# Attention scores as pairs of 64-row TensorE tiles, with unpadded keys and another share-out of PSUM

## Chip, cores, metric

One core of a Trainium2 chip. The metric is the device time of one execution in microseconds, slowest core (here the only one). The kernel before: 403.52 us, median of 4 runs (401.85 to 407.54).

## The reference, cut to what matters

```python
# batch 8, heads 8, 576 positions, head_dim 64; d_model 512, d_ff 2048
scores = q @ k^T / 8 + bias_table[bucket(|i - j|)]     # per batch and head
attn   = softmax(scores) @ v
x      = attn.transpose(0, 2, 1, 3).reshape(4608, 512)
h      = x @ w_in
out    = (h + sin(alpha * h)**2 / alpha) @ w_out
```

## The kernel before

Everything is fp16 with fp32 accumulation. A planner in Python keeps a list of tasks per engine and emits them in the order of a modelled time, so each engine's instruction order is fixed when the kernel is built. Three kinds of work share TensorE (PE below): **scores** and attention times values (**av**) of batch t; **hidden** matmuls (x by w_in) of a block of 512 rows; and **mo** matmuls (g by w_out, where g is h + sin(alpha * h)**2 / alpha), which have the lowest priority and go wherever nothing else is ready. The vector engine (DVE) applies the bias and does most of the copying. The exp runs on the scalar engine (ACT) in an *exp stage* per batch, the sine in a *sin stage*; a table load lies between them.

The heads have 64 channels, but the array has 128 rows. Two heads lie above one another in a tile of 128 partitions, and the keys are padded with zeros, so that one 128-row matmul gives one head's scores:

```python
# kz: [128, 4 pairs, 2*576]; head 0 in rows 0..63 of the first half, head 1 in rows 64..127 of the second
units = [(0, c) for c in range(4)] + [(1, 0), (2, 0), (2, 2)]     # 7 a pair of heads
for z in range(2):                                                # a unit fills one two-bank PSUM tile
    for y in range(1 if kind == 0 else 2):
        k0 = S * z + 128 * (c + y)
        q0, n = WIN[0 if kind == 0 else 1]                        # WIN = ((0, 384), (384, 192))
        full(sc.v[:, z, n*y : n*y + n], kz[:, p, k0 : k0 + 128], qT[:, p, q0 : q0 + n], True, True)
...
nc.scalar.activation(out=o, in_=x, func=AF.Exp, scale=0.125)      # one exp of 768 a unit, 576 for the tail
```

The last 64 keys of both heads (the *tail*, `kt`) share one 128-row matmul. PSUM: two score tiles of two banks each, two banks for av, two for mo. In the sin stages the score banks hold the hidden matmuls' results.

The softmax here doesn't subtract the row's maximum and nothing guards it: scores larger than these inputs give would overflow.

Of the kernel before, what the change touches and what calls it, by code (L numbers as in the profile page):

```python
# [34 lines left out]
NBUF = {"sc": 4, "av": 2, "mo": 2, "u": 3, "g": 2, "s16": 3, "sq": 3, "outs": 5, "xn": 3, "xp": 5}  # L35


class Task:
    def __init__(self, engs, emit, deps, pri, nb=0.0):
        self.engs, self.emit, self.deps, self.pri, self.nb = engs, emit, list(deps), pri, nb  # L40
        self.allocs = []
        self.s_only = self.fill = False
        self.end = self.eng = None


class Buf:
    def __init__(self, tag):
        self.tag, self.users = tag, []
# [6 lines left out]
class Plan:  # L55


    def __init__(self):
        self.tasks = []
        self.sin = self.in_qk = False  # L60
        self.used = self.share = 0
        self.warm = None
        self.rings = {k: [] for k in NBUF}

# [9 lines left out]
    def ready(self, t):  # L74
        r = t.nb
# [8 lines left out]
        for b in t.allocs:  # L84
            ring, n = self.rings[b.tag], NBUF[b.tag]
            k = taken[b.tag] = taken.get(b.tag, -1) + 1
            if len(ring) + k >= n:
                for x in ring[k - n].users:
                    if x.end is None:
                        return None  # L90
                    r = max(r, x.end)
        return r

    def run(self, t0):
        free = {e: t0 for e in ("PE", "ACT", "DVE", "POOL", "DMA", "SP")}
        todo = list(self.tasks)
        while todo:
# [30 lines left out]
            if e == "PE" and self.warm is not None and free[e] < WARM_END:  # L128
                ring = self.rings["mo"][-2:]
                b = Buf("mo")  # L130
                x = Task({}, None, [], 0)
                b.users.append(x)
                if st > free[e] + 0.5 and len(ring) == 2 and all(
# [5 lines left out]
                    self.rings["mo"].append(b)  # L139
                    continue  # L140
            if t.fill:
                self.used += 1
                st -= FILL_GAP
                fin -= FILL_GAP
            for b in t.allocs:
                self.rings[b.tag].append(b)
# [13 lines left out]
D_FLIP = 3.0  # L160
T_START = 7.0
# [30 lines left out]
def kernel(  # L192
# [46 lines left out]
    kzs = [sgl.tile([128, NP, 2 * S], F16, name=f"kz{i}") for i in range(2)]  # L239
    kraw = sgl.tile([128, NP, S], F16, name="kraw")  # L240
# [75 lines left out]
    banks = [0]  # L316
    halves = {}

    def new_sc(n):
        z = banks[0] // 2 % 2  # L320
        m, pool = halves.get(z, (0, None))
        if m != n:
            if pool is not None:
                pool.release()
            pool = tc.alloc_tile_pool(
                name=f"sc{banks[0]}", bufs=1, space=bass.MemoryType.PSUM,
                side="right" if z else "left", reuse_waits="tile",
            )
            halves[z] = (n, pool)
        banks[0] += n  # L330
        if n == 1:
            return pool.tile([128, 512], F32, name="sc", tag="sc", bufs=2)
        return pool.tile([128, 2, 512], F32, name="sc", tag="sc", bufs=1)

    def new_av():
        return ps.tile([128, 512], F32, name="av", tag="av", bufs=NBUF["av"])

    def new_mo():
        return ps.tile([128, 512], F32, name="mo", tag="mo", bufs=NBUF["mo"])
# [8 lines left out]
    def load_kqT(t):  # L348
        nc.sync.dma_start_transpose(out=kraw[:, :, :], in_=staged_k.ap()[t])
        kz = kzs[t % 2]  # L350
        nc.sync.dma_start(out=kz[0:64, :, 0:S], in_=kraw[0:64, :, :])
        nc.sync.dma_start(out=kz[64:128, :, S : 2 * S], in_=kraw[64:128, :, :])
        for z in range(2):
            r = slice(64 * z, 64 * z + 64)
            nc.sync.dma_start(out=kts[t % 2][r, :, r], in_=kraw[r, :, 512:S])
        nc.sync.dma_start_transpose(out=qTs[t % 2][:, :, :], in_=staged_q.ap()[t])

# [47 lines left out]
    def clear(eng, i):  # L405
        eng.memset(kzs[i][0:64, :, S : 2 * S], 0.0)
        eng.memset(kzs[i][64:128, :, 0:S], 0.0)
# [11 lines left out]
    def warm(n):  # L419
        x = new_mo()  # L420
# [53 lines left out]
    eps_ = new_mo()  # L474
# [34 lines left out]
    def plan_tr(t, p, kq, pri, nb, deps=()):  # L509

        b, c = Buf("mo"), Cell()
        far = kq == 0 and (t == 1 or p > FAR)

        def mm(e):
            c.v = new_mo().bitcast(F16)
# [15 lines left out]
        def cp(e):  # L531
            pin = c.v[:, 0:S].rearrange("d (i p) -> d p i", i=SI)

            def put(dst, r):
                copy_on(e, dst.rearrange("d (p i) -> d p i", i=SI)[r], pin[r])

            if kq == 1:
                put(qTs[t][:, p, :], slice(0, 128))
            elif far:
                put(kraw[:, p, :], slice(0, 128))  # L540
            else:
                put(kzs[t][:, p, 0:S], slice(0, 64))
                put(kzs[t][:, p, S : 2 * S], slice(64, 128))

        m = plan.add({"PE": 0.4 if t == 0 and p == 0 else 0.5}, mm, deps, pri, nb, new=[b])
        eng = {"DVE": 0.75, "ACT": 0.72} if kq or far else {"DVE": 1.6, "ACT": 1.55}
# [5 lines left out]
        if far:  # L552
            farq.append((p, x))
            if t and p % 2 == 0:
                return [], []
# [4 lines left out]
            def split(e):  # L560
                kz = kzs[t]
                nc.sync.dma_start(out=kz[0:64, p0:p1, 0:S], in_=kraw[0:64, p0:p1, :])
                nc.sync.dma_start(out=kz[64:128, p0:p1, S : 2 * S], in_=kraw[64:128, p0:p1, :])
                for z in range(2):
                    r = slice(64 * z, 64 * z + 64)
                    nc.sync.dma_start(out=kts[t][r, p0:p1, r], in_=kraw[r, p0:p1, 512:S])
# [4 lines left out]
            return [y], [y]  # L571

        def tail(e):
            for z in range(2):
                r = slice(64 * z, 64 * z + 64)
                nc.vector.tensor_copy(
                    out=kts[t][r, p, r], in_=kzs[t][r, p, S * z + 512 : S * z + S]
# [4 lines left out]
    def plan_alpha():  # L582
        b, c = Buf("mo"), Cell()

        def mm(e):
            c.v = new_mo()
# [14 lines left out]
    def plan_pair(t, p, kqt, tails, first, gate, ub):  # L601

        u = Cell()
        done = {}
        units = [(0, c) for c in range(4)] + [(1, 0), (2, 0), (2, 2)]
        head = []
        for i, (kind, c) in enumerate(units):
            b, sc = [Buf("sc"), Buf("sc")], Cell()

            def qk(e, i=i, kind=kind, c=c, sc=sc):  # L610
                if i == 0:
                    if p == 0:
                        first()
                        plan.in_qk, plan.used = True, 0
                        plan.quota = QUOTA.get(t, QUOTA_ELSE)
                    u.v = new_u()
                plan.share = (len(units) * p + i + 1) / (NP * len(units))
                if p == NP - 1 and i == len(units) - 1:
                    plan.in_qk = False
                sc.v = new_sc(2)  # L620
                kz, qT = kzs[t % 2], qTs[t % 2]
                for z in range(2):
                    if kind == 1:
                        full(sc.v[:, z, 0:288], kts[t % 2][:, p, :],
                             qT[:, p, 288 * z : 288 * z + 288], True, True)
                        continue
                    for y in range(1 if kind == 0 else 2):
                        k0 = S * z + 128 * (c + y)
                        q0, n = WIN[0 if kind == 0 else 1]
                        full(sc.v[:, z, n * y : n * y + n], kz[:, p, k0 : k0 + 128],  # L630
                             qT[:, p, q0 : q0 + n], True, True)

            def ex(e, kind=kind, c=c, sc=sc):
                uz = u.v[:, 0:8, :].rearrange("p (z c) q -> p z c q", z=2)
                if kind == 0:
                    o, x = uz[:, :, c, 0:384], sc.v[:, :, 0:384]
                elif kind == 1:
                    o = u.v[:, 8, :].rearrange("p (b q) -> p b q", b=2)
                    x = sc.v[:, :, 0:288]
                else:  # L640
                    o = uz[:, :, c : c + 2, 384:576]
                    x = sc.v[:, :, 0:384].rearrange("p z (c q) -> p z c q", c=2)
                nc.scalar.activation(out=o, in_=x, func=AF.Exp, scale=0.125)  # L643

            base = PB + 100 * (16 * p + 2 * i)
            n = 576 if kind == 1 else 768
            m = plan.add({"PE": n / 2400.0 + 0.01}, qk, kqt + (tails if kind == 1 else []), base,
                         after=head + (list(split_of.values()) if t == 1 else [])
                         + ([aheads[t]] if t in aheads else []), new=b + ([ub] if i == 0 else []))
            head = head or [m]  # L650
            qk_last[:] = [m]
            x = plan.add({"ACT": t_act(n)}, ex, [m] + gate, base + 20, use=b + [ub])
            if kind == 1:

                def bh(e):
                    io = u.v[:, 8, 384:576]
                    nc.vector.tensor_tensor(out=io, in0=io, in1=mh[:, p, 0:192], op=ALU.mult)

                done[(0, 4)] = x
                done[(1, 4)] = plan.add({"DVE": 0.19}, bh, [x], base + 10,  # L660
                                         nb=0.0 if t else T_MH[p > 0], use=[ub])
                continue
            w = 0 if kind == 0 else 1
            q0, n = WIN[w]
            for cc in range(c, c + 1 + w):
                done[(w, cc)] = x
                lo, hi = max(q0, 128 * cc - 128), min(q0 + n, 128 * cc + 256)
# [299 lines left out]
```

## Time and profile before

| | before |
|---|---|
| time, median of 4 | 403.52 us |
| span of the profiled execution | 400.6 us |
| PE / ACT / DVE busy | 97% / 83% / 67% |
| exp stage, batches 4 to 7 | 21.8 us |
| sin stage, batches 3 to 6 | 17.5 us |
| last stretch, after the last exp | 103.8 us |

The prediction below shows the lines of these views. One excerpt more, PE's timeline in an exp stage (start, duration, instruction, count): how a pair's last scores lie among the filler.

```profile
284.42 0.49 PE L417 MATMUL sc<-qT,kz 128*128 128x192 f16 x4
284.75 0.59 PE L417 MATMUL mo<-w_out,g 128*128 128x512 f16 x2
285.18 0.49 PE L417 MATMUL sc<-qT,kz 128*128 128x192 f16 x4
285.51 0.38 PE L417 MATMUL mo<-w_out,g 128*128 128x512 f16 x1
```

A row's duration includes the pipeline's end; what an instruction costs PE is the distance between starts. Four score matmuls of 192 columns take 284.75 - 284.42 = 0.33 us, 82 ns each; the mo matmul from 285.51 is followed at 285.73, 0.22 us later. There is no gap.

### The profile page before, as it was taken

Reading aid. Unit: us, or ns where it says so; the run is one execution under the profiler, and the core shown is the slowest. Engines: PE = TensorE matmul, PEld = TensorE weight load, DVE = VectorE, ACT = ScalarE, POOL = GpSimd, SP = SyncE. Lnnn points to the kernel's source line nnn. Section 1 sums busy time; section 2 is a strip of 40 time slices with the busy share of each in tenths; the row PEclk is TensorE's granted clock in tenths of the full one; section 3 lists DMA queues with packets and bytes.
Section 4 is the critical chain, followed back from the end, with each engine's and each line's share of the span. In section 5 each row is a group of like instructions: output and inputs, shape, how many; then the busy total and the mean of one; then the engine's idle time right before and its main releaser. Section 6 shows DMA issues by size and latency. Waiting matters only on the chain.

```text
span 400.6 us, 8664 instructions
## 1 busy us (share of the span) xinstructions
PE 388.1 (97%) x3398; PEld 221.9 (55%) x3398; DVE 266.5 (67%) x621; ACT 331.6 (83%) x492; POOL 86.2 (22%) x98
## 2 busy tenths in 40 slices
PE   5989999999999999999999999999999999999996
PEld 2466447744777744774477447745764444444442
DVE  5886976777676778678866877687766808519200
ACT  2888999889999999999999999999996818729311
POOL 7962944170009080009000400000000000000000
PEclk9999999999999999999999999999999999999999
DMA  9999999999929999989971946200131020010122
GB/s 169 214 214 221 215 188 142 188 179 156 210 59 110 183 185 155 128 175 128 165 187 33 101 94 167 57 16 28 45 57 41 2 79 26 19 65 22 54 79 79
DMA packets 152808, 46.42 MB, mean 116 GB/s; under 512 B 138104, under 2 KB 147152, under 8 KB 152768
## 3 DMA queue, kind: packets, MB, share of 16 engines
q0 software_dynamic: 89872, 19.04, 57.7%
q1 hardware_dynamic: 62672, 26.79, 32.4%
q8 instruction: 26, 0.43, 0.4%
q14 instruction: 14, 0.11, 0.1%
q10 hardware_dynamic: 224, 0.05, 0.1%
HBM read 37.76 MB, written 16.52 MB: 136 GB/s over the span
## 4 chain that ended last, share of the span: by engine, by line
PE 86%; DMA 5%; ACT 5%; DVE 2%; issue 1%; POOL 0%; ACTq 0%; SPq 0%; DVEq 0%
PE sc L417 44%; PE mo L417 30%; PE av L417 11%; DMA kz<-kraw 2%; ACT s L805 2%; DMA e_dram<-e_sb 1%; DMA phi_sb<-phi_const 1%; ACT u L643 1%; DMA mhr<-e_dram 1%; ACT sq L812 1%; DVE g L819 1%; PE av L764 0%; DVE sq L814 0%; ACT L875 0%; DVE u L674 0%
## 5 line engine op out<-in xcount | busy, mean ns | idle before, releaser
L643 ACT ACTIVATE u<-sc 128x768 f16<-128x768 f32 (+1 forms) x224 | 162.1, 788 | 6.8 <-PE sc L417 4.4
L417 PE MATMUL mo<-w_out,g 128*128 128x512 f16 x576 | 152.6, 379 | 0.0
L417 PE MATMUL sc<-xT,w_in 128*128 128x512 f16 x576 | 132.4, 379 | 0.2 <-DVE g L819 0.2
L819 DVE SCALAR_TENSOR_TENSOR g<-sq,inv_a,sc 128x512 f16<-128x512 f16 x144 | 103.7, 746 | 35.1 <-PE mo L417 25.8
L417 PE MATMUL sc<-qT,kz 128*128 128x192 f16 (+1 forms) x512 | 94.9, 289 | 3.9 <-ACT u L643 1.5
L805 ACT ACTIVATE s<-sc,alphaT 128x512 f16<-128x512 f32 x144 | 93.0, 678 | 6.2 <-PE sc L417 4.9
L674 DVE TENSOR_TENSOR u<-u,m2r 128x512 f16<-128x512 f16 (+1 forms) x192 | 68.8, 389 | 44.0 <-ACT u L643 43.5
L417 PEld LDWEIGHTS <-w_in 128*128 128x128 f16 x576 | 55.1, 98 | 64.3 <-issue 0.5
L417 PEld LDWEIGHTS <-g 128*128 128x128 f16 x576 | 55.8, 98 | 50.8
L417 PEld LDWEIGHTS <-u 128*128 128x128 f16 x1440 | 61.7, 97 | 12.0 <-DVE u L674 0.2
L417 PEld LDWEIGHTS <-kz 128*128 128x128 f16 x512 | 43.3, 98 | 29.4 <-issue 7.4
L417 PE MATMUL av<-v,u 128*128 128x65 f16 x1280 | 59.3, 193 | 0.0
L812 ACT ACTIVATE sq<-s 128x512 f16<-128x512 f16 x78 | 49.0, 629 | 2.8 <-DVE g L819 0.7
L361 POOL DMA_DIRECT2D v<-in_v_dram x24 | 22.2, 1060 | 116.8 <-PE av L417 116.8
L503 ACT ACTIVATE outs<-mo 128x512 f32<-128x512 f32 x18 | 10.7, 597 | 41.7 <-PE mo L417 41.7
L417 PE MATMUL av<-vh,u 128*128 128x130 f16 x160 | 35.1, 220 | 0.0
L814 DVE TENSOR_TENSOR sq<-s 128x512 f16<-128x512 f16 x66 | 27.8, 423 | 8.6 <-ACT s L805 7.8
L727 DVE TENSOR_TENSOR xp<-av,rd 128x384 f16<-128x384 f32 (+1 forms) x48 | 23.6, 491 | 1.7
L875 ACT ACT_TABLE_LOAD x13 | 16.7, 1283 | 0.2
L343 POOL DMA_DIRECT2D staged_q<-in_q_dram x6 | 16.1, 2680 | 1.5 <-DMA staged_q<-in_q_dram 1.5
L726 DVE RECIPROCAL rd<-av 128x6 f32<-128x6 f32 x64 | 11.9, 186 | 4.8 <-PE av L417 4.0
L343 POOL DMA_DIRECT2D staged_k<-in_k_dram x6 | 13.5, 2254 | 3.3 <-DMA staged_k<-in_k_dram 3.3
(74 smaller groups left out, 140.6 us busy)
## 6 DMA issues: line engine op xcount, KB each, us to landing
out_dram<-outs SPq DMA_DIRECT2D x36, 256.0 KB, 2.0
staged_k<-in_k_dram POOLq DMA_DIRECT2D x6, 576.0 KB, 13.2
staged_q<-in_q_dram POOLq DMA_DIRECT2D x6, 576.0 KB, 17.3
kz<-kraw SPq DMA_DIRECT2D x12, 288.0 KB, 6.6
v<-in_v_dram POOLq DMA_DIRECT2D x24, 128.0 KB, 6.5
w_in<-in_moe_w_in_dram POOLq DMA_DIRECT2D x4, 512.0 KB, 8.4
w_out<-in_moe_w_out_dram POOLq DMA_DIRECT2D x4, 512.0 KB, 12.0
w_out<-in_v_dram SPq DMA_DIRECT2D x4, 256.0 KB, 8.7
```

The source lines that it names most:

```text
L343: nc.gpsimd.dma_start(out=dst.ap()[t].rearrange("s (h d) -> s h d", h=H), in_=src[t].rearrange("h s d -> s h d"),)
L361: nc.gpsimd.dma_start(out=vs[t % 2][:, c, :, 0:D], in_=vp[128 * c : 128 * c + 128],)
L417: nc.tensor.matmul(out=out, lhsT=lhsT, rhs=rhs, start=start, stop=stop)
L643: nc.scalar.activation(out=o, in_=x, func=AF.Exp, scale=0.125)
L674: nc.vector.tensor_tensor(out=io, in0=io, in1=m2[:, 2 * p : 2 * p + 2, x0 : x0 + hi - lo], op=ALU.mult,)
L726: nc.vector.reciprocal(out=r, in_=a[:, :, :, D])
L727: nc.vector.tensor_tensor(out=y.rearrange("p c (z d) -> p c z d", z=2), in0=a[:, :, :, 0:D], in1=r.unsqueeze(3).to_broadcast([128, nq, 2, ...
L805: nc.scalar.activation(out=s16.v, in_=h.v, func=AF.Sin, scale=alphaT[:, f : f + 1])
L812: nc.scalar.activation(out=sq.v, in_=s16.v, func=AF.Square)
L814: k_of(e).tensor_tensor(out=sq.v, in0=s16.v, in1=s16.v, op=ALU.mult)
L819: nc.vector.scalar_tensor_tensor(out=gcell[b].v[:, f, :], in0=sq.v, scalar=inv_a[:, f : f + 1], in1=h.v, op0=ALU.mult, op1=ALU.add,)
L875: nc.scalar.preload_act_table_set(name)
```

## The change

Intent: a 64-row matmul uses half of the array, and two on different halves can run together. So each head's scores are computed from its own 64 partitions, without zero padding, and both heads of a unit run side by side. That also does away with the padded copy of the keys. A switch between the full array and row tiles costs something, so from batch 2 on two units are issued as a run; this needs a third score tile, which is taken from the av and mo banks. Units become 512 queries (four a pair) and 64 queries (one a pair), plus the tail.

```diff
-    kzs = [sgl.tile([128, NP, 2 * S], F16, name=f"kz{i}") for i in range(2)]
-    kraw = sgl.tile([128, NP, S], F16, name="kraw")
+    kTs = [sgl.tile([128, NP, S], F16, name=f"kT{i}") for i in range(2)]
     def load_kqT(t):
-        nc.sync.dma_start_transpose(out=kraw[:, :, :], in_=staged_k.ap()[t])
-        kz = kzs[t % 2]
-        nc.sync.dma_start(out=kz[0:64, :, 0:S], in_=kraw[0:64, :, :])
-        nc.sync.dma_start(out=kz[64:128, :, S : 2 * S], in_=kraw[64:128, :, :])
+        kT = kTs[t % 2]
+        nc.sync.dma_start_transpose(out=kT[:, :, :], in_=staged_k.ap()[t])
...
+        if t < LAG - 1:                                   # LAG = 3: batches 0 and 1
+            groups = [[(p, i)] for p in range(NP) for i in (0, 1, 2, 3, "t", 4)]
+            nreg = 2
+        else:
+            groups = [
+                [(y + p, i) for y, i in g] for p in range(0, NP, 2) for g in (
+                    ((0, 0), (0, 1)), ((0, 2), (0, 3)), ((0, "t"),), ((0, 4), (1, 0)),
+                    ((1, 1), (1, 2)), ((1, "t"),), ((1, 3), (1, 4)),
+                )
+            ]
+            nreg = 3
...
+                    for y in range(1 if i < 4 else 4):
+                        q0, n = QW[i == 4]                # QW = ((0, 512), (512, 64))
+                        k0 = 128 * (i if i < 4 else y)
+                        for z in range(2):
+                            r = slice(64 * z, 64 * z + 64)
+                            full(sc.v[:, z, n * y : n * y + n], kT[r, p, k0 : k0 + 128],
+                                 qT[r, p, q0 : q0 + n], True, True)
...
-        mb, ob, m = Buf("mo"), Buf("outs"), Cell()
+        mt = "moE" if b == 0 else "am" if b < T - 2 else "moL"
+        mb, ob, m = Buf(mt), Buf("outs"), Cell()
...
+        if t == LAG - 1:
+            early = early + cps[0] + avs[1] + xdone[(1, 0)] + xdone[(1, 1)]
```

`am` is either of two banks that av and mo share from batch 2 on; `moE` and `moL` are two banks before and three after that time. The last two lines mean that batch 2's scores come only after block 0's mo and batch 1's av are done, because they take over those banks.

## The prediction

> **What bounds the kernel now.** I read the page first: how full each engine is, and who makes the chain that ended last.
>
> ```profile
> PE 388.1 (97%) x3398; PEld 221.9 (55%) x3398; DVE 266.5 (67%) x621; ACT 331.6 (83%) x492; POOL 86.2 (22%) x98
> PE 86%; DMA 5%; ACT 5%; DVE 2%; issue 1%; POOL 0%; ACTq 0%; SPq 0%; DVEq 0%
> L643 ACT ACTIVATE u<-sc 128x768 f16<-128x768 f32 (+1 forms) x224 | 162.1, 788 | 6.8 <-PE sc L417 4.4
> L417 PE MATMUL sc<-qT,kz 128*128 128x192 f16 (+1 forms) x512 | 94.9, 289 | 3.9 <-ACT u L643 1.5
> ```
>
> TensorE makes 86% of the chain. ACT at 83% looks far behind, but that is an average over unlike stages. So next I cut the span at the 13 table loads (each marks a change between an exp stage and a sin stage) and read the busy time of each stretch.
>
> ```profile
> core 0: us, PE busy (x) PEld busy (x) DVE busy (x) ACT busy (x) POOL busy (x), PEclk, DMA share, GB/s
> 235.70:257.50 21.80, 21.80 (x267) 15.07 (x265) 14.55 (x42) 21.53 (x29) 0.00 (x0) 1.00 0.51 125
> 257.50:275.00 17.50, 17.50 (x106) 8.38 (x103) 14.78 (x27) 17.04 (x28) 0.00 (x0) 1.00 0.09 17
> 296.80:400.60 103.80, 100.12 (x486) 45.58 (x482) 45.52 (x80) 54.50 (x88) 0.00 (x0) 1.00 0.14 46
> ```
>
> A batch is an exp stage of 21.8 us and a sin stage of 17.5 us. In both, PE and ACT are full together. The last stretch, 104 us, has PE full and ACT at half. A matmul's shown duration includes its pipeline, so I counted PE work by start-to-start times in the trace: 216 ns for 512 columns, 162 for 384, 122 for 288, 82 for 192, 29 for an attention matmul of 65. In the exp stage from 235.7 that gives scores 8.5 us, attention times values 5.2 and 35 output matmuls (mo) 7.55: 21.2 of 21.8, only 0.5 us unused. The sin stage: 64 hidden matmuls 13.8, 13 mo 2.8, the rest 1.0. So 48 mo are done per batch, while 64 come due; the backlog waits, and from 296.8 on PE works off 192 hidden and 268 mo matmuls (41.4 + 57.6 us). **The mo matmuls are filler**: PE issues them wherever scores wait for ACT. Hence the reading that decides all: PE time saved in an exp stage does not shorten that stage, which ACT paces, but lets more mo in and shortens the tail, 0.216 us each. Up to 76 mo of the first six blocks are still undone at 296.8, so there is room for that.
>
> **What the skill says.** "TensorEngine Tiling (Array Packing)", Tiling Modes, Key Properties: tiles work independently, and changing the tiling mode drains the engine. The trace of before shows both, in the transposes of batch 1, which run as 96*64 column tiles between full matmuls:
>
> ```profile
> 42.22 1.03 PE L417 MATMUL sc<-xT,w_in 128*128 128x512 f16 x4
> 43.17 0.45 PE L525 MATMUL mo<-id_sb,nat 96*64 96x96 f16 x12
> 43.55 1.04 PE L417 MATMUL sc<-xT,w_in 128*128 128x512 f16 x4
> 44.52 0.45 PE L525 MATMUL mo<-id_sb,nat 96*64 96x96 f16 x12
> 44.90 2.79 PE L417 MATMUL sc<-xT,w_in 128*128 128x512 f16 x12
> ```
>
> From 43.55 to 44.52 four matmuls of 216 ns (0.864) take about 0.966: going in costs 0.09-0.10. The twelve transposes start in pairs 3 ns apart, a pair per 43 ns, the first pair per 66, and the next full matmul starts 138 ns after the last transpose instead of 43. Sum of the excess: 92 + 23 + 95 = **0.21 us per excursion** into another mode and back. "TensorE: Matmul & The Clock Gate", Part 3: packing four 32-row tiles with 512 columns gave 3.07 times the speed; no row tile runs in the kernel before, so for two 64-row tiles I take the column tiles' behaviour. "TensorEngine Tiling", Gotcha 1: row tiles write different PSUM banks and need more PSUM; the change pays just that. "ScalarE: Activation LUTs", What ACT_TABLE_LOAD costs: 0.833 ns per element plus a fixed part. This trace has exps back to back at 690 ns for 768 and 531 for 576 columns, that is 0.83 ns each plus 50 ns.
>
> **Part 1, scores on PE.** Before, a head pair takes 8 x 162 + 8 x 82 + 2 x 122 ns = 2.20 us, 8.78 a batch. After: four units of two concurrent 512-column tiles, 4 x 0.22 = 0.88; the 64-query unit, four concurrent pairs at about 43 ns = 0.17 (estimate from the transposes' pairs; 0.23 if its eight weight loads go one by one at 29 ns); the tail, unchanged in full mode, 0.244. Sum 1.29, or 5.18 a batch. To that come the excursions. Filler lies between any two groups, so every row-tiled group is one. Batches 0 and 1: five a pair, 20 a batch, 4.2 us, total 9.4: **0.6 us dearer** than before. From batch 2, in runs of two units: five per two pairs, 10 a batch, 2.1 us, total 7.3: **1.5 us saved**. That is why the runs begin there.
>
> **Part 2, where it counts.** Batches 3 to 7 have PE full: 5 x 1.5 = 7.5 us, some 35 mo moved out of the tail. In batch 2 (97 to 119) PE has 2.0 us unused already, since the filler quota of that batch is 30: nothing gained. Batch 1: 0.6 lost. Batch 0 has PE gaps: nothing lost.
>
> **Part 3, exp on ACT.** Before, a pair's floor is 6 x 690 + 531 = 4.67 us; after, 4 x 903 + 531 + 477 = 4.62. Nothing to win. The stage takes 5.1 a pair today; with three tiles and runs of two, a run after a short exp (tail or 64 queries) must wait for the exp before that: about 0.3 us three times per two pairs, 0.5 a pair, as much as today. Such waits are filled with mo.
>
> **Part 4, start.** The copy of padded keys (two of 756 ns per pair on DVE, pairs 0 and 1) becomes one, and pairs 2 and 3 no longer wait for the kz<-kraw transfers:
>
> ```profile
> 19.64 8.36 DMA kz<-kraw
> 28.05 0.66 PE L417 MATMUL sc<-qT,kz 128*128 128x384 f16 x3 [0.41 <-DMA kz<-kraw]
> 28.42 0.81 ACT L643 ACTIVATE u<-sc 128x768 f16<-128x768 f32 x1 [0.62 <-PE sc L417]
> ```
>
> ACT idles 3.9 us between 8.5 and 28.5; I expect 1.0 us back, because the bias tables (landed at 18.1) hold the attention of pair 0 anyway.
>
> **Part 5, PSUM.** From batch 2 scores take six banks and attention and mo share two instead of four. From the trace, a mo bank is held 8 to 14 us in an exp stage and an attention bank 1.5 to 2.8; more than two are held at once 8 to 11% of the exp stage. So filler is missing at times: I take 0.3 us of PE idle per stage, 1.5 in all. Batch 2 may also start only after block 0's mo copies: before, 4 of its 64 mo were left at 96.9; 0.7 lost.
>
> **Sum.** 7.5 - 0.6 + 1.0 - 1.5 - 0.7 = 5.7 us saved; 403.5 - 5.7 = **397.8 us** (-1.4%).
>
> **Rivals.** (a) *The filler is lost to the two shared banks*: mo holds one bank nearly always, attention turns over the other, and in the new order both attention windows of a pair come late and together. If PE idles 1.5 us a stage, the gain is gone: 403 to 404. For it: four banks become two. Against: the 8 to 11% above. (b) *The switch is cheap or groups join*: if the mode change costs half, 1.05 us a batch more is saved from batch 3 on, and batch 1 breaks even or better: about 392. For it: row tiles load weights of full width, unlike the transposes. Against: the drain is of the full matmul before, which stays. (c) *Row tiles do not run together*: then scores cost 4.2 us more a batch, and with the switches the time is above 418. Against it: the 3 ns between paired transposes. (d) *Exp stages lengthen* by the waits of Part 3: harmless while mo is there to fill, since PE sets the total.
>
> **Range and chances.** The main term, 7.5, has about 4 us either way from switch cost and the 64-query unit; the banks 3 us, mostly one way; the start 1 us. Eight in ten: 391 to 404. Two per cent is below 395.5, which needs (b) or no bank loss: 0.34. Slower needs (a) at its worst or (c): 0.06.
>
> **What will show it.** Right: pairs of score matmuls starting a few ns apart, next pair 216 to 220 ns later; about 0.1 us more at each border of row-tiled groups; mo in the exp stages of batches 3 to 7 about 42 instead of 35; the last stretch about 7 us shorter, with the stage lengths as before; no kz<-kraw transfer. Wrong: PE gaps above 1 us in an exp stage with mo or attention waiting for a PSUM copy (a); borders under 0.05 us (b); 216 ns between the two tiles of a pair (c); exp stages changed by more than 1 us, which would mean that ACT's waits and not PE's work set the total.

## The result

392.81 us, median of 4 (392.0 to 393.95). Ratio 0.9722, 95% interval 0.9646 to 0.9799. A ratio is the mean time of one kernel's fast runs over that of the other's in the same rounds, so it is not quite the ratio of the medians. Executions over 1.5% slower than the fastest of the same kernel are left out of the means. Faster, by 10.7 us in the medians; the forecast was 5.7, inside its range, and its chance of more than 2% was 0.34.

The page after the change, with the rows that answer those of before:

```profile
PE 378.4 (96%) x3401; PEld 190.1 (48%) x3401; DVE 262.0 (67%) x587; ACT 323.9 (83%) x458; POOL 81.9 (21%) x96
PE 86%; DMA 4%; DVE 4%; ACT 3%; POOL 1%; issue 1%; ACTq 0%; DVEq 0%
L705 ACT ACTIVATE u<-sc 128x1024 f16<-128x1024 f32 (+1 forms) x192 | 157.8, 898 | 14.4 <-PE sc L450 12.9
L450 PE MATMUL sc<-qT,kT 64*128 64x64 f16 (+1 forms) x512 | 50.8, 297 | 1.7 <-ACT u L705 0.9
```

The score row fell from 94.9 to 50.8 us busy; the exp row is 4 us shorter, but waits for scores 12.9 us in place of 4.4. The busy time of the stages (columns as in the prediction's table: stretch, length, then busy time of PE, weight loads, DVE, ACT, POOL):

```profile
237.14:259.59 22.45, 22.38 (x259) 11.53 (x258) 14.68 (x39) 20.86 (x26) 0.00 (x0) 1.00 0.44 106
259.59:277.17 17.58, 17.58 (x121) 8.79 (x120) 14.46 (x27) 17.19 (x29) 0.00 (x0) 1.00 0.13 33
299.66:392.20 92.54, 88.59 (x449) 40.74 (x447) 44.68 (x78) 53.21 (x87) 0.00 (x0) 1.00 0.12 44
```

The exp stage is not shorter but 0.6 us longer, and the last stretch is 11.3 us shorter. Counted by start times in the trace, 213 mo matmuls are left for it in place of 268, 55 x 0.216 = 11.9 us. PE's timeline in an exp stage shows the runs:

```profile
276.79 1.46 PE L450 MATMUL am<-w_out,g 128*128 128x512 f16 x6
278.18 0.60 PE L450 MATMUL sc<-qT,kT 64*128 64x512 f16 x4
278.72 1.47 PE L450 MATMUL am<-w_out,g 128*128 128x512 f16 x6
280.12 0.61 PE L450 MATMUL sc<-qT,kT 64*128 64x512 f16 x4
...
282.95 0.51 PE L450 MATMUL sc<-qT,kT 64*128 64x64 f16 x10
283.39 0.23 PE L450 MATMUL am<-vh,u 128*128 128x130 f16 x1
```

Six mo from 276.79 would end at 278.09 (6 x 0.216); the run starts at 278.18, so going in costs 0.09. Four matmuls of 512 columns, in two pairs with starts 3 ns apart, should take 0.44 and take 0.54: coming out costs another 0.09. Over all such borders in the trace: 311 ns and 308 ns in place of 216, so **0.187 us an excursion**. The four pairs of 64-query matmuls between 282.95 and the next 512-column pair take 0.126 us: their starts are 39, 29, 29 and 29 ns apart. Over a batch in runs, scores now cost PE 6.9 us with all excursions (3.46 for two pairs of heads, from the starts: three runs of 0.635, two mixed ones of 0.535, two tails of 0.244), against 8.8 before.

**A ledger of PE.** I added up, from the trace, what each matmul should cost (216, 162, 122 and 82 ns for 512, 384, 288 and 192 columns, as read above; in between along the line through these, 0.417 ns a column plus 2.5; at least 29; 220 and 27 ns for a pair of row tiles; 0.187 an excursion) and took the rest as time not at work. The changed kernel's trace here is that of the control run e10. (A 64-column pair takes 29 to 32 ns rather than 27; that would move 0.6 us of the changed kernel from time not at work to scores.)

| us | before | changed (e10) |
|---|---|---|
| span | 400.6 | 391.8 |
| scores | 70.6 | 39.4 |
| excursions (transposes of the start included) | 1.9 | 18.1 |
| all work | 376.3 | 362.1 |
| not at work: to the end of sin stage 0 | 16.1 | 18.7 |
| batch 1 | 0.3 | 1.1 |
| exp stages 2 and 3 | 2.3 | 2.2 |
| from there to the last exp | 1.7 | 3.4 |
| last stretch | 3.9 | 4.3 |

Work fell by 14.2 us, of which 5.4 came back as idle time, half of that in the start. A column-tiled and a row-tiled group next to each other are counted as one excursion: 97 in e10, of which 60 lie in the batches with runs. The span of the profiled run of before is one of its quicker ones; see "What stays open".

### The profile page after: what moved, and what is told of

It is laid out like the page before. It is cut to its first block, busy times and chain, and to the rows that moved or that the text cites. A ratio compares the mean times of both kernels' runs of the same rounds, so it can differ in the third digit from the quotient of the medians.

```text
span 392.2 us, 8566 instructions
## 1 busy us (share of the span) xinstructions
PE 378.4 (96%) x3401; PEld 190.1 (48%) x3401; DVE 262.0 (67%) x587; ACT 323.9 (83%) x458; POOL 81.9 (21%) x96
## 4 chain that ended last, share of the span: by engine, by line
PE 86%; DMA 4%; DVE 4%; ACT 3%; POOL 1%; issue 1%; ACTq 0%; DVEq 0%
PE sc L450 41%; PE am L450 34%; PE cb L450 5%; PE ca L450 5%; ACT u L705 2%; DMA m2r<-e_dram 2%; DMA e_dram<-e_sb 1%; DMA phi_sb<-phi_const 1%; DVE g L879 1%; DVE u L730 1%; ACT s L865 1%; DVE xn L785 1%; DVE outs L538 0%; DVE kT L538 0%; POOL mhr L471 0%
## 5 line engine op out<-in xcount | busy, mean ns | idle before, releaser
L705 ACT ACTIVATE u<-sc 128x1024 f16<-128x1024 f32 (+1 forms) x192 | 157.8, 898 | 14.4 <-PE sc L450 12.9
L450 PE MATMUL am<-w_out,g 128*128 128x512 f16 x416 | 108.6, 380 | 0.3 <-DVE outs L538 0.2
L730 DVE TENSOR_TENSOR u<-u,m2r 128x512 f16<-128x512 f16 (+2 forms) x160 | 67.7, 438 | 32.4 <-ACT u L705 27.8
L450 PEld LDWEIGHTS <-u 128*128 128x128 f16 x1440 | 55.8, 98 | 19.2 <-issue 11.0
L450 PE MATMUL sc<-qT,kT 64*128 64x64 f16 (+1 forms) x512 | 50.8, 297 | 1.7 <-ACT u L705 0.9
L450 PE MATMUL am<-v,u 128*128 128x65 f16 x1152 | 51.2, 194 | 0.0
L450 PE MATMUL am<-vh,u 128*128 128x130 f16 x144 | 32.2, 224 | 0.8 <-DVE xp L785 0.8
L450 PEld LDWEIGHTS <-kT 64*128 64x128 f16 x512 | 14.7, 96 | 28.5 <-issue 24.3
L785 DVE TENSOR_TENSOR xp<-am,rd 128x384 f16<-128x384 f32 (+1 forms) x48 | 23.6, 491 | 1.8
L450 PE MATMUL cb<-w_out,g 128*128 128x512 f16 x96 | 23.0, 380 | 0.0
L538 DVE COPY outs<-am 128x512 f32<-128x512 f32 x19 | 13.1, 688 | 4.3 <-PE am L450 4.1
## 6 DMA issues: line engine op xcount, KB each, us to landing
w_out<-in_moe_w_out_dram POOLq DMA_DIRECT2D x4, 512.0 KB, 10.7
```

The costliest lines, as they stand in the source:

```text
L450: nc.tensor.matmul(out=out, lhsT=lhsT, rhs=rhs, start=start, stop=stop)
L538: k_of(e).tensor_copy(out=o, in_=i)
L730: nc.vector.tensor_tensor(out=io, in0=io, in1=m2[:, 2 * p : 2 * p + 2, x0 : x0 + hi - lo], op=ALU.mult,)
L785: nc.vector.tensor_tensor(out=y.rearrange("p c (z d) -> p c z d", z=2), in0=a[:, :, :, 0:D], in1=r.unsqueeze(3).to_broadcast([128, nq, 2, ...
```

## The experiments

The theory after the result: **the total is the sum of PE's work, and scores with their excursions shrank.** Rivals: the larger exp units do it; the excursions are hidden; the shared PSUM banks eat part of the gain; filler placement, not work, decides.

### e1, runs undone

```diff
-            groups = [ [(y + p, i) ...] for p in range(0, NP, 2) for g in (((0, 0), (0, 1)), ...) ]
+            groups = [[(p, i)] for p in range(NP) for i in (0, 1, 2, 3, "t", 4)]
             nreg = 3
```

(abridged)

> The changed kernel with its runs of two undone: from batch 2 on each unit is a group of its own, still on three score tiles and with the two shared banks. Theory (TensorE's work sets the total, and each excursion into row tiles costs it 0.19 us, as the trace of the changed kernel shows at its borders): 20 excursions a batch in place of 10, 1.9 us more in each of five or six full batches, so 9 to 11 us more than the changed kernel: 402 to 404 us. Rival (the concurrency of the tiles is the gain, the excursions fall into time in which TensorE would wait anyway): 393 to 395.

Measured: 405.16 us, ratio 0.9996 (0.9926 to 1.0066). Against the changed kernel's 0.972 that is 11 us, the total that was expected, and the rival falls; but 60 excursions more, 11.2 us, is not how it came about. In the trace many neighbouring single units have no filler between them and share an excursion: 131 in all, 34 more than in e10, or 6.4 us. The spans differ by 10.8 us; by the same ledger the other 4.5 are PE not at work (34.1 us in place of 29.6), 1.2 to 1.8 us in each exp stage from batch 4 on. There ACT is busy for 20.19 of 20.22 us, so in this run it is ACT that paces the stage. 281 mo matmuls were left for the last stretch, which took 107.8 us. The clean count of excursions is in e2.

### e2, two tiles and own banks throughout

```diff
-        if t < LAG - 1:
+        if True:                                    # groups of one, nreg = 2
-        at = "avE" if t < LAG - 1 else "am"
+        at = "avE"
-        mt = "moE" if b == 0 else "am" if b < T - 2 else "moL"
+        mt = "moE"
```

(abridged; batch 2's wait for block 0's mo and batch 1's av goes too)

> The arrangement of batches 0 and 1 for all batches: single units on two score tiles, attention and output matmuls with two banks each. Theory: the scores of a batch cost 8.7 us of TensorE, as in the kernel before (8.8), so 401 to 404, and within 1.5 us of the run with single units on three tiles. Rival (the two shared banks cost much): clearly faster than that run, by 3 us or more.

Measured: 403.79 us, ratio 0.9963 (0.9897 to 1.0029), 1.4 us under e1 in the same rounds, intervals overlapping. Here single units stay apart: 156 excursions, 59 more than in e10, are 11.0 us, and the run is 11.0 us slower than the changed kernel (403.79 against 392.81); PE not at work is 28.2 us in place of 29.6. So runs are worth the 11 us, and single row-tiled units, unpadded keys included, gain nothing over padded full matmuls: what the concurrency gives, the switch takes. The pair of e1 and e2 does not price the banks: e2 has 25 excursions more and yet 5.9 us less of PE not at work, and two things differ, the number of score tiles and the banks. The banks are tested in e11.

### e3, heads in turn within a run

```diff
-                        for z in range(2):          # innermost: heads alternate
+                for z in range(2):                  # outermost: head 0 of both units, then head 1
```

(abridged)

> The changed kernel with the order of the matmuls inside a run turned: both units of head 0 first, then both of head 1, so that only the middle two of four 512-column matmuls lie on different row tiles one after the other. Theory (two row tiles run together, and that is what saves): each run of two units takes three steps of 216 ns in place of two, 10 runs a batch, 2.2 us more a batch in six batches; single units are unchanged: 403 to 406 us. Rival (the gain is of the unit sizes and of the unpadded keys, not of the concurrency): under 395.

Measured: 398.1 us, ratio 0.9826 (0.975 to 0.9901): 4 us over the changed kernel, not 11. The expectation failed because the edit did not do what it was meant to. PE's timeline of this run:

```profile
280.34 0.61 PE L450 MATMUL sc<-qT,kT 64*128 64x512 f16 x4
280.88 1.47 PE L450 MATMUL am<-w_out,g 128*128 128x512 f16 x6
...
289.27 0.74 PE L450 MATMUL sc<-qT,kT 64*128 64x512 f16 x10
289.94 0.82 PE L450 MATMUL am<-w_out,g 128*128 128x512 f16 x3
```

The run of two units still takes 0.54 us. Its four starts are at 280.341, 280.348, 280.567 and 280.573: two at once, though the program has both matmuls of head 0 first, and two on one tile start 217 ns apart (e5). So the third in the program started before the second. The semaphore operations in the trace agree: the second and the fourth start are those that signal a finished score tile, which in the program are the third and the fourth matmul. Only the mixed run (five matmuls of one head in a row) lost: 0.67 us in place of 0.44; there head 1's first start came 0.23 us after head 0's. Four such runs a batch cost 4 x 0.23 = 0.9 us, in six batches 5.5, about the 4 measured. The question was put again in e5.

### e4, the new units in the kernel before

```diff
-        units = [(0, c) for c in range(4)] + [(1, 0), (2, 0), (2, 2)]
+        units = [(0, c) for c in range(4)] + [(1, 0), (2, 0)]     # 512 queries, tail, 64 queries x 4 chunks
```

(and the windows of exp, bias and the waits of av as in the changed kernel; padded keys, full matmuls)

> The kernel before, padded keys and full-array matmuls, with units of 512 and 64 queries in place of 384 and two of 192, and attention waiting as in the changed kernel. Theory: TensorE's columns are the same (8 x 216 + 8 x 29 + 2 x 122 ns a pair, 2.2 us), and the total is TensorE's: 400 to 405. Rival (fewer exp instructions with larger units, six a pair in place of seven, are part of the gain): 398 or less.

Measured: 408.63 us, ratio 1.0074 (1.0007 to 1.0142), above the expected 400 to 405. A steady period (two table loads of the same kind apart) takes 39.19 us, before 39.28: the units change nothing there. The loss is in the start: the first sin table load is at 39.0 us in place of 34.2. PE's score matmuls wait 3.0 us for `kz<-kraw` transfers in place of 0.4, and after those waits the granted clock is 0.52 from 25 to 30 us and 0.80 from 30 to 35, where before has 1.00. How much each of the two costs is not separated. The rival falls: unit size alone brings no gain.

### e5, both heads on one row tile

```diff
                             r = slice(64 * z, 64 * z + 64)
+                            r = slice(0, 64)        # wrong heads on purpose
```

> Wrong result on purpose: both heads of a unit read rows 0 to 63 of keys and queries, so the two matmuls of every pair lie on the same row tile and cannot run together; number, shapes, score banks and order are those of the changed kernel. The run before with the heads turned round did not take the concurrency away (the trace still showed two starts a few ns apart). Theory (the tiles' concurrency is the gain): 16 x 216 + 16 x 27 ns = 3.9 us more a batch, and TensorE is full in six to seven batches: 20 to 27 us more than the changed kernel, ratio to the kernel before 1.02 to 1.04. Rival (score time was hidden beside exp, the gain comes from elsewhere): ratio under 0.99.

Measured: 424.44 us, ratio 1.0516 (1.0413 to 1.0618). (The comparison with the reference still passed; probably the scores are so small with these inputs that its tolerance does not see the wrong head. So a passed comparison does not vouch for the scores here.) PE's timeline:

```profile
304.45 1.03 PE L450 MATMUL sc<-qT,kT 64*128 64x512 f16 x4
305.42 1.47 PE L450 MATMUL am<-w_out,g 128*128 128x512 f16 x6
```

The run takes 0.97 us in place of 0.54, the pairs being one after the other. The kernel loses (1.0516 - 0.9722) x 403.5 = 32 us, more than expected: 3.9 us in **all eight** batches would be 31 us. In the ledger, which still counts pairs as concurrent, the rest grows by 4.9 us in the start, 3.1 in batch 1, 7.2 in batches 2 and 3 and 15.2 in batches 4 to 7. This settles the concurrency as the cause, and shows that added PE work counts nearly in full in every batch.

### e6, less filler in the exp stages

```diff
-QUOTA_ELSE = (8, 48)
+QUOTA_ELSE = (6, 24)
```

The quota is the planner's limit on mo matmuls in a batch's *score window*, between its first and last score matmul: it starts at the first number and grows by the second as the scores are issued.

> The changed kernel with the filler quota of the exp stages lowered from 8 + 48 to 6 + 24 output matmuls, so that from batch 4 on at most 30 of them (the changed kernel has 36 to 42) lie between a batch's first and last score matmul. Theory (saved TensorE time counts only because output matmuls move out of the last stretch): the 30 to 40 held back come at the end again, 0.216 us each, less what the sin stages take: 5 to 8 us lost, ratio 0.984 to 0.992. Rival (shorter score work shortens the exp stages themselves): the exp stages get shorter still with less filler, ratio 0.97 or lower.

Measured: 395.06 us, ratio 0.9756 (0.9686 to 0.9826), between the two expectations and not clearly apart from the changed kernel (2.3 us above it in device time). The stages tell more than the time:

```profile
233.17:254.19 21.02, 20.66 (x250) 10.80 (x249) 14.51 (x39) 20.52 (x26) 0.00 (x0) 1.00 0.50 113
254.19:271.00 16.81, 16.81 (x117) 8.41 (x116) 15.17 (x28) 16.41 (x27) 0.00 (x0) 1.00 0.13 34
292.02:393.70 101.68, 97.71 (x491) 44.94 (x489) 45.12 (x80) 54.34 (x88) 0.00 (x0) 1.00 0.13 47
```

There are 29 mo in a score window in place of 36 to 42. The exp stage is 1.4 us shorter, and the last stretch, with 255 mo, 9.1 us longer. Held-back filler moves the time about and hardly changes the sum. So the rival is right that the stage follows the filler, and wrong that this sets the total. The prediction's view, that only mo moved out of the tail counts, is too narrow.

### e7 and e11, two shared banks in the kernel before

```diff
-    NBUF "av": 2, "mo": 2                            # two banks each
+    at = "avE" if t < LAG - 1 else "am"              # from batch 2 both use the banks am0, am1
+    mt = "moE" if b == 0 or b >= T - 2 else "am"
```

(abridged; the first line is put in words)

> The kernel before with its score tiles and padded keys as they are, but attention and output matmuls sharing two PSUM banks from batch 2 on, as in the changed kernel (two banks lie unused). Measures what the change pays in PSUM. The prediction's step: 0.3 us a stage and 0.7 at batch 2, together 2.2 us: ratio 1.003 to 1.008. Rival (mo holds one bank nearly always, so attention starves the filler): 7 us or more, ratio over 1.017.

Measured: 421.92 us, ratio 1.0425 (1.0348 to 1.0502), far over both expectations. But the loss is one wait, not the banks:

```profile
95.62 0.38 PE L432 MATMUL am<-w_out,g 128*128 128x512 f16 x1
110.14 0.80 PE L432 MATMUL sc<-qT,kz 128*128 128x384 f16 x2 [14.14 <-DMA qT<-staged_q]
```

Batch 2's first score matmul is held up 14 us by a transfer of queries; the SP queue's timeline has only batch 3's transfer landing then. In my edit those loads came ahead of the matmul in the program. e11 repeats it with one line that puts the loads behind:

```diff
+            if t == LAG - 1 and p == 0 and not head:
+                aheads[t + 1].after.append(m)
```

> The earlier run with two shared banks in the kernel before, mended: there batch 2's first score matmul came behind the loads of batch 3 in the program and waited 14 us for one of them, which is no cost of the banks. Here those loads are issued behind it. Its steady batches took 39.15 us with the same 48 output matmuls as before, so the theory that two banks suffice expects a ratio of 0.998 to 1.010; the rival (shared banks starve the filler) 1.017 or more.

Measured: 404.69 us, ratio 1.0042 (0.9972 to 1.0113), and a steady period of 39.16 us:

```profile
203.62:242.78 39.16, 39.16 (x366) 23.49 (x365) 29.89 (x72) 37.35 (x55) 4.78 (x6) 1.00 0.93 111
```

Before it is 39.28. Two banks for av and mo cost a steady batch nothing. (Earlier in this trace, batch 4's first score matmul waits 2.0 us; the cause is not settled.) For the order of the changed kernel its own trace speaks: PE is busy for 22.38 of 22.45 us in the exp stage above, and in e10's ledger it is not at work for 0.5 to 0.8 us per exp stage from batch 4 on, before 0.5 to 0.6. Rival (a) needs 1.5 us a stage, so it falls.

### e8, no quota

```diff
-QUOTA = {2: (4, 26)}; QUOTA_ELSE = (8, 48)
+QUOTA = {2: (8, 48)}; QUOTA_ELSE = (16, 96)
```

> The changed kernel with the filler quota raised to 16 + 96 (batch 2: 8 + 48). If the quota still holds filler back, the last stretch loses up to 21 output matmuls more (4.5 us): ratio 0.961 to 0.968. If time and banks limit the filler, not the quota: 0.970 to 0.975, as the changed kernel.

Measured: 394.44 us, ratio 0.9745 (0.9661 to 0.9829); 215 mo after the last score matmul, the same number as in the changed kernel. In batch 2 the quota did hold filler back (40 mo in its score window now, 29 with the quota), but batch 3 then has 20 in place of 28: it only shifts the 128 that exist by then.

### e9, e10 and e12: runs from batch 1 on

e9 sets the border between single units and runs at batch 1, with the transposes and av of batch 0 ahead of it; e10 is the changed kernel unaltered.

```diff
-        if t < LAG - 1:
+        if t < 1:
-        mt = "moE" if b == 0 else "am" if b < T - 2 else "moL"
+        mt = "am" if b < T - 2 else "moL"
```

> The changed kernel with runs of two units and shared banks from batch 1 on in place of batch 2. Theory (the total is the sum of TensorE's work, wherever it lies): 10 excursions of 0.19 us fewer in batch 1, 1.9 us, and batch 2 starts without the change of banks; 1 to 3 us under the changed kernel in the same rounds. Rival (batch 1's transposes of its own output need the banks, so filler and attention stall there): the same or slower.

> The changed kernel unaltered, as the control of this call: ratio 0.970 to 0.976.

Measured: e10 392.53 us, ratio 0.972 (0.967 to 0.977); e9 395.03, ratio 0.978 (0.9733 to 0.9826). PE's work is 1.9 us less in e9's ledger, and yet the kernel is 2.5 us slower. Exp stages 2 and 3, first the changed kernel, then e9:

```profile
96.75:140.69 43.94, 43.00 (x544) 22.74 (x542) 29.57 (x81) 40.27 (x50) 9.23 (x8) 1.00 0.98 102
```

```profile
99.31:141.11 41.80, 38.36 (x521) 21.69 (x520) 29.71 (x82) 39.89 (x50) 9.24 (x8) 1.00 1.14 108
```

PE has 3.4 us without any matmul in place of 0.9. No sin stage lies between batches 2 and 3, so until its end only the 128 mo of blocks 0 and 1 exist, and e9 has used more of them in batch 1 (14 in batch 3's score window in place of 28). In the changed kernel, too, all 128 are gone when batch 3's scores end; before, 14 were left. e12 holds some of them back:

```diff
+QUOTA = {1: (6, 20), 2: (4, 26)}                     # on top of e9
```

> Runs of two from batch 1 on, as in the earlier run that was 2.5 us slower than the changed kernel, and the filler quota of batch 1 lowered to 6 + 20. In that run the 128 output matmuls of blocks 0 and 1 were used up before batch 3 ended (14 in batch 3's score window in place of 28) and TensorE stood idle 3.4 us in batches 2 and 3 in place of 0.9. If that is why it lost, holding 17 of them back in batch 1 gives the time back, and the 1.9 us of saved excursions shows: ratio 0.964 to 0.970, under the changed kernel's 0.972. Rival (batch 1 itself suffers from the two shared banks): 0.975 to 0.981.

Measured: 393.89 us, ratio 0.9714 (0.9656 to 0.9772): by the ratio the loss of e9 is gone, by the device times about half of it (395.03, here 393.89, e10 392.53), and the hoped-for gain did not come. (In this call the kernel before was at the upper of its two levels in 6 of 11 runs, see "What stays open", which flatters the ratio.) The ledger has 1.7 us less work and 1.9 us more idle time than e10. That fits a front part of the kernel (to the end of batch 3) which has no more filler to take up time saved there; what else sets its length is not settled. None of the twelve runs beat the changed kernel clearly.

## Why the prediction was right, and by how much it was off

The mechanism was right: concurrency less excursions, spent on filler, seen at the end. The size was half of the measured one. By its own parts:

- **Part 1, scores.** Forecast 7.3 us a batch in runs, measured 6.9; so 1.9 saved in place of 1.5. Two terms were too high: the excursion (0.21 from the column tiles, 0.187 for row tiles) and the 64-query unit (0.17, measured 0.13). For batches 0 and 1 "0.6 dearer" was 0.2: a single 512-query unit takes 0.418 us with its excursion and a single 64-query unit 0.319, so 16 x 0.418 + 4 x 0.319 + 4 x 0.244 = 8.9 against 8.8. That single units gain nothing was right (e2).
- **Part 2, where it counts.** The forecast counted five batches at 1.5. Batch 2 with "nothing gained" was wrong: by the end of batch 3 the changed kernel had done all 128 mo of the first two blocks and the old one 114. In the ledger batches 2 and 3 together gain 3.5 us, close to twice 1.9. "ACT paces the stage" failed in e6: with less filler the stage is shorter (21.0 us). ACT sets a floor near 20.2 us (e1), but in the changed kernel PE is what fills the stage. The sum of PE's work is what holds.
- **Part 3, exp.** Right that exp gains nothing (e4's steady period). Its 531 ns for an exp of 576 columns is no distance between starts in the trace of before, where the least is 630; the changed kernel's trace has 530. The stage grew by 0.6 to 1.0 us with waits for scores, and as rival (d) said this was harmless.
- **Part 4, start.** The forecast 1.0 was wrong in the traces. The first exp stage does end earlier, by 0.7 us in the first trace of the changed kernel (33.6 against 34.2; its granted clock was 0.66 between 25 and 30 us) and by 1.4 in e10's (32.9, clock 1.0). But all 45 av matmuls of its last pair then lie in the sin stage, in place of 18, and the end of sin stage 0 came later: 55.8 and 55.4 against 54.6.
- **Part 5, PSUM.** The third score tile pays for the runs, not for the row tiles themselves: e2 has row tiles on two score tiles. 2.2 us were charged. e11's steady period shows no cost; from the end of batch 3 to the last exp the ledger has 3.4 us of PE not at work in place of 1.7; the cause of these 1.7 us is not settled. The wait of batch 2 for block 0's mo exists (ACT idles 1.9 us there), but PE is full of mo meanwhile.

The sum, stretch by stretch from the traces of before and e10 (how much shorter the stretch became, plus the mo and other work done in it that lay later before): start to the end of sin stage 0 -0.8, batch 1 -0.2, batches 2 and 3 +3.5, batches 4 to 7 +6.8, last stretch -0.4: 8.8 us, the difference of the two spans. Against the forecast's 5.7, the main misses are batch 2, the cheaper excursion and the PSUM charge, all to one side, and the start to the other. Rival (b)'s figure, 392, came true, but its cause did not: the switch is not cheap. Rival (c)'s 4.2 us a batch comes out as 3.6 from the prediction's own terms (four pairs of heads, each 8 x 0.216 + 8 x 0.029 in place of 0.88 + 0.17); e5 showed 3.6 to 4.0 in batches 2 to 7.

**What stays open.** The kernel before has two levels: of 40 runs, 19 lie at 401.6 to 404.1 and 18 at 406.2 to 408.7. The changed kernel's ten lie at 391.8 to 394.0. Two variants with padded keys (e4, e11) were traced with a first sin table load near 39 us; their score matmuls wait 3.0 and 3.3 us for `kz<-kraw`, and the granted clock falls to 0.52 and 0.66 between 25 and 30 us. The trace of before has 34.2, 0.4 and 1.00. So the upper level may be those transfers landing late, and the change, which has none, would be rid of it. No trace of the kernel before at its upper level was taken, so this is not shown. It would explain why the medians differ by 10.7 us and the traces by 8.8. The mean granted clock does not tell the levels apart (407.83 us at 1.0, 402.99 at 0.981). The mean of the kernel before's fast runs lies between 403.6 and 405.7 us in the experiments, so ratios can be apart by 0.5% for this alone.

## What to carry to other kernels

Where low-priority work fills every gap of a full engine, add up that engine's work over the whole kernel, each switch included: stage lengths only tell where the time lies. Check too whether filler exists in the part where time is saved; without it, saved time turns into idle time. A mode switch has to be divided by the work done between two switches, so group first: here single units gave back all that the concurrent tiles saved, and runs of two kept 2.8%.

## What the Trainium skill lacked or had wrong

- "TensorEngine Tiling (Array Packing)", Tiling Modes, Key Properties: it says that a mode switch drains the engine, without a cost. Here: 95 ns going into 64-row tiles and 92 ns coming out, on top of a 512-column matmul's 216; 0.21 us an excursion for column-tiled transposes.
- "TensorE: Matmul & The Clock Gate", Part 3: it calls matmuls strict FIFO in start and end. In e3 the third matmul in program order, on the other row tile, started 7 ns after the first and 0.22 us before the second. The reach is short: behind five of one tile, the other tile's first start came 0.23 us late.
- The same part says that weight loads overlap matmuls in flight only when the row group differs. In the changed kernel the second pair's loads (278.189 and 278.192, the same two row groups) start 11 ns after the first pair's matmuls, which stream until 278.40; the loads for the full-array mo matmuls do the same (278.727, 11 ns after the mo matmul at 278.716). The mechanism paragraph of the same part names the background weight buffer as a second way, and that would fit.
- For two 64-row tiles "TensorEngine Tiling (Array Packing)", Theoretical Speedup, has only "Up to 2×", and no page has a measurement. Here pairs of 512 columns start 227 ns apart (278.179 and 278.406 in the changed kernel) against 216 for full matmuls one by one, and pairs of 64 columns 29.
